# A decode-attention kernel on one core: shorter ScalarE and VectorE programs, the last V load in two pieces, 64-column pick matmuls, and the output weights in pieces of 16/8/5/2/1 and groups of eight

## The chip, the cores and the metric

The kernel runs on one core of a Trainium2 chip. The metric is device time in microseconds (us). Times are medians of several executions. All runs told here were classed as fast, so no slow-state run is compared with a fast one. The profiled execution is one of the timed ones, and its "span", the time from its first to its last instruction, is 1.4 to 2.0 us shorter than its device time. Times inside a profile count from the start of the span. A load "lands" when the profile shows its completion. The clock records here know two states of TensorE: full clock (1.00) and half clock (0.50).

## The reference, cut to what matters

```python
x: (1, 1, 512)   k_cache, v_cache: (1, 32, 16384, 128)   wq: (512, 4096)   wo: (4096, 512)   # all bf16
g = sigmoid((x * gate_w).sum(-1))
q = (x @ wq) in 32 heads of 128
a = (softmax(q k^T * 128**-0.5) v) in one row of 4096, @ wo        # per head, 16384 keys
b = gMLP(x) with w_in (512, 1792), w_out (896, 512)                # small
return g * a + (1 - g) * b                                         # one row of 512
```

One query row reads the whole of K and V: 268 MB of the 279.6 MB that the kernel moves. There is little arithmetic for each byte.

## The kernel before

K and V are loaded in sixteen pairs of heads, 8.4 MB for a K or a V load, into three big buffers of 64 KB per partition. For a pair, VectorE multiplies K by q in place in four chunks, TensorE adds up over d with an identity matrix, VectorE reduces to scores, ScalarE takes the exponentials, and TensorE multiplies with V. A load that reuses a buffer is issued only when that buffer's last user has finished.

The sizes of the pieces at the end of the stream:

```python
WG = 4                                   # rows of wo in one group of the "wide" part
TG = 8                                   # V matmuls in one group; NT = 8 groups for a pair
V_CUTS = (0, 160, 224, 256)              # last V load: pieces of 160, 64 and 32 keys per partition
WO_CUTS = (0, 16, 24, 28, 31, 32)        # wo: 16, 8, 4, 3, 1 rows per partition
WIDE = 16
```

Which buffer a load waits for (`n` counts loads; K of pair 0, K of pair 1, V of pair 0, K of pair 2, V of pair 1, ...):

```python
    for n, kind, i in loads:
        wait = [user[n - 3]] if n >= 3 else [w_free] if buf[n % 3] is setup else []
        ...
        if i == NP - 1:
            cuts, sems = (K_CUTS, ld_kh) if kind == "k" else (V_CUTS, ld_vp)
        for a, b, done in zip(cuts[:-1], cuts[1:], sems):
            sp.op(lambda e, ...: e.dma_start(...), wait=wait if a == 0 else (), inc=(done, 16))
```

V on TensorE, then the "pick" matmuls, which gather eight partial rows into two columns of the output:

```python
    def values(e, p, pa, va):
        ...
        with e.Fori(0, NT) as t:
            ...                                  # TG matmuls of 512 columns, after v_s
            fill(e, 8)
        o2 = o_ps[:, bass.ds(value(e, p, NP - 1) * 2, 2)]
        fill(e, 8, 2)
        take(e, drn_s)                           # ScalarE has drained d_ps to d_sb
        for r in range(4):
            ins = e.matmul(o2, lhsT=d_sb[:, r * Dh:(r + 1) * Dh], rhs=pick[:, r * 2:(r + 1) * 2], ...)
```

The exponentials, the drain, and the pair loop on ScalarE:

```python
    def exps(e, i):
        take(e, red_s)
        ...                                      # two Exp activations of 64x256, with sums into L_sb
    def act_pairs(e):
        e.wait_ge(*p_zero)
        exps(e, 0)
        exps(e, 1)
        with e.Fori(2, NP) as i:
            renew(e)                             # drain d_ps to d_sb, zero d_ps
            exps(e, i)
        renew(e)
        ...
```

The tail: normalise, transpose and reorder the output (VectorE and TensorE in turns), then 16 rows of wo as "wide" matmuls in a loop of WIDE / WG groups, then the other 16 rows one by one as their pieces land. (`fill` adds matmuls whose results nobody uses, to keep TensorE busy.) A piece of wo is waited for only ahead of its own rows:

```python
        with e.Fori(0, WIDE // WG) as t:
            ...                                  # WG matmuls 1x512, after wo_s
            fill(e, 1)
    for j, (a, b) in enumerate(zip(WO_CUTS[:-1], WO_CUTS[1:])):
        for k in range(max(a, WIDE), b):
            y_ok = add(o2[:, k:k + 1], wo[:, k * D:(k + 1) * D], [(ld_o[j], 16)] if k == a else (), ...)
        if b == 24:
            add(ones_f[:, 0:1], d_sb[:, :], [w_ok])     # the wide part's sum
```

The softmax here doesn't subtract the row's maximum and nothing guards it: scores larger than these inputs give would overflow.

Of the kernel before, what the change touches and what calls it, by code (L numbers as in the profile page):

```python
# [5 lines left out]
ACT = mybir.ActivationFunctionType  # L6
ALU = mybir.AluOpType
AX = mybir.AxisListType

FP32 = mybir.dt.float32  # L10
BF16 = mybir.dt.bfloat16

P = 128
Dh = 128
H = 32
NP = H // 2
# [15 lines left out]
NS = Dh // W  # L32
NG = KP // 4
TG = 8
WG = 4
NT = NG // TG
ZB = F // 4
K_CUTS = (0, 128, 256)
V_CUTS = (0, 160, 224, 256)
WO_CUTS = (0, 16, 24, 28, 31, 32)  # L40
WIDE = 16
inv_sqrt_dh = float(Dh) ** -0.5


# [132 lines left out]
def gated_mix_kernel(nc, A_x, A_k_cache, A_v_cache, A_wq, A_wo, B_x, B_w_in, B_w_sp, B_b_sp,  # L177
                     B_w_out, gate_w, out):
    def sb(name, shape, dt):
        return nc.alloc_sbuf_tensor(name, shape, dt)  # L180
# [4 lines left out]
    p_t = sb("p_t", [P, 2 * NG * 8], BF16)  # L185
    s_sb = sb("s_sb", [P, KP], FP32)
    d_sb = sb("d_sb", [P, 512], FP32)
    zero = sb("zero", [P, 512], BF16)
# [6 lines left out]
    ident = sb("ident", [P, P], BF16)  # L195
    eps_t = sb("eps_t", [P, 1], FP32)
    sel = sb("sel", [H, 4 * (P + 1)], BF16)
    pick = sb("pick", [P, 4 * 2], FP32)
    wbf = sb("wbf", [P, 2], FP32)
    g_sb = sb("g_sb", [P, 1], FP32)  # L200
    gm_sb = sb("gm_sb", [P, 1], FP32)
# [6 lines left out]
    var = sb("var", [P, 1], FP32)  # L208
    rstd = sb("rstd", [P, 1], FP32)
    u = sb("u", [P, FhC], BF16)  # L210
    L_sb = sb("L_sb", [P, H], FP32)
    rl = sb("rl", [P, H], FP32)
    o_sb = sb("o_sb", [P, H], BF16)
    oT = sb("oT", [H, P], BF16)
    o2 = sb("o2", [P, H], BF16)
# [6 lines left out]
    g_ps, t_ps = l_ps[:, 0:3], s_ps[0][:, 0:2]  # L222
# [19 lines left out]
    ld_x, ld_g, ld_q, ld_w, ld_u, st_out = (  # L242
        sem(n) for n in ("ld_x", "ld_g", "ld_q", "ld_w", "ld_u", "st_out"))
# [12 lines left out]
    pool, sp, pe, dve, act = (Queue(nc, e, n) for e, n in (  # L256
        (nc.gpsimd, "pool"), (nc.sync, "sp"), (nc.tensor, "pe"), (nc.vector, "dve"),
        (nc.scalar, "act")))


    def counter(e, name, value):
        reg = e.alloc_register(name)
        e.reg_mov(reg, value)
        return reg

    def value(e, reg, top):
        return nc.snap(bass.RegisterHandles([reg]), min_val=0, max_val=top)
# [4 lines left out]
    ident_ok = pool.chain(lambda e: e.affine_select(  # L272
        out=ident[:, :], in_=ident[:, :], compare_op=ALU.not_equal, fill=1.0, base=0,
        pattern=[[-1, P]], channel_multiplier=1))
    for t in [L_sb, p_t, zero]:
        p_zero = pool.op(lambda e, t=t: e.memset(t[:, :], 0.0), mark=True)
    pool.raw(lambda e: e.nop().then_inc(exp_s, 1))
    const_ok = dve.op(lambda e: e.memset(sel[:, :], 0.0), mark=True)


    act.op(lambda e: e.dma_start(out=x_row[:, :], in_=A_x.rearrange("b s d -> (b s) d")),
# [14 lines left out]
    for c in range(DC):  # L296
        x_ok = pe.op(lambda e, c=c: e.matmul(
            m_ps[1][:, c * P:(c + 1) * P], lhsT=x_row[0:1, c::DC], rhs=ones_row[0:1, :],
            start=True, stop=True), wait=[(ld_x, 16)] if c == 0 else (),
            mark=(c == DC - 1))  # L300
# [4 lines left out]

    act.op(lambda e: e.copy(
        out=sel[:, :].rearrange("h (i x) -> h i x", x=P + 1)[:, :, 0:P:4],
        in_=ident[0:H, 0:H].unsqueeze(1).broadcast_to([H, 4, H])), wait=[const_ok, ident_ok],
        mark=True)
    dve.op(lambda e: e.tensor_reduce(  # L310
        out=pick[:, :].rearrange("p (r s) -> p s r", r=4),
        in_=ident[:, :].rearrange("p (g x) -> p x g", x=32)[:, 0:8, :]
        .rearrange("p (s r) g -> p s r g", r=4), axis=AX.X, op=ALU.add), wait=[ident_ok], mark=True)
    dve.op(lambda e: e.tensor_tensor(out=xg_row[:, :], in0=x_row[:, :], in1=gw_row[:, :],
                                     op=ALU.mult), wait=[(ld_x, 16), (ld_g, 48)], mark=True)
    dve.op(lambda e: e.tensor_copy(out=xgw[:, 1:3], in_=wb_row[:, :]), mark=True)
    xgw_ok = dve.chain(lambda e: e.tensor_reduce(out=xgw[:, 0:1], in_=xg_row[:, :], axis=AX.X,  # L317
                                                 op=ALU.add))
# [3 lines left out]
                                    stop=True), wait=[xgw_ok], mark=True)  # L322
    act.op(lambda e: e.activation(out=g_sb[:, :], in_=g_ps[:, 0:1], func=ACT.Sigmoid),
           wait=[g_ok], mark=True)
    gm_ok = act.op(lambda e: e.activation(out=gm_sb[:, :], in_=g_ps[:, 0:1], func=ACT.Sigmoid,
                                          scale=-1.0), mark=True)
    dve.op(lambda e: e.tensor_copy(out=wbf[:, :], in_=g_ps[:, 1:3]), wait=[gm_ok], mark=True)
    g_free = dve.chain(lambda e: e.memset(g_ps, 0.0))



# [47 lines left out]
    for h in range(2):  # L379
        zh = ps_all[:, 6 * h * 512:(6 * h + 2) * 512].rearrange("p (b x) -> p b x", b=2)[:, :, 0:ZB]  # L380
        dve.op(lambda e, h=h, zh=zh: e.tensor_tensor(  # L381
            out=zm[:, 2 * h * ZB:2 * (h + 1) * ZB].rearrange("p (b m k) -> p b m k", b=2, k=FhC),
            in0=zh.rearrange("p b (m k) -> p b m k", k=FhC),
            in1=ident[:, :].rearrange("p (b m) -> p b m", b=2).unsqueeze(3).broadcast_to(
                [P, 2, 64, FhC]), op=ALU.mult), wait=[z_ok] if h == 0 else (), mark=True)
    zm_ok = (dve.sem, dve.n)
    dve.chain(lambda e: e.tensor_reduce(
        out=z[:, :].rearrange("p (e k) -> p e k", e=2),
        in_=zm.rearrange("p (e m k) -> p e k m", e=2, k=FhC), axis=AX.X, op=ALU.add))
    dve.chain(lambda e: e.scalar_tensor_tensor(  # L390
        out=zt[:, :], in0=z[:, :], scalar=0.044715, in1=z[:, :], op0=ALU.mult, op1=ALU.mult))
    zt_ok = dve.chain(lambda e: e.scalar_tensor_tensor(
        out=zt[:, :], in0=zt[:, :], scalar=1.0, in1=z[:, :], op0=ALU.add, op1=ALU.mult))
# [3 lines left out]
                  mark=True)  # L397
    dve.op(lambda e: e.tensor_tensor(out=z[:, :], in0=z[:, :], in1=zt[:, :], op=ALU.mult),
           wait=[sg_ok], mark=True)
    dve.chain(lambda e: e.tensor_reduce(out=stats[:, 0:1], in_=z[:, FhC:FC], axis=AX.X, op=ALU.add))  # L400
    dve.op(lambda e: e.tensor_tensor(out=sq[:, :], in0=z[:, FhC:FC], in1=z[:, FhC:FC],
                                     op=ALU.mult), mark=True)
    st_ok = dve.chain(lambda e: e.tensor_reduce(out=stats[:, 1:2], in_=sq[:, :], axis=AX.X,
                                                op=ALU.add))
    tot_ok = pe.op(lambda e: e.matmul(t_ps, lhsT=ones_f[:, :], rhs=stats[:, :],
                                      start=True, stop=True), wait=[st_ok], mark=True)
    dve.op(lambda e: e.tensor_scalar(out=mv[:, :], in0=t_ps, scalar1=1.0 / Fh,
                                     scalar2=0.0, op0=ALU.mult, op1=ALU.add), wait=[tot_ok],
           mark=True)
    var_ok = dve.chain(lambda e: e.scalar_tensor_tensor(  # L410
        out=var[:, :], in0=mv[:, 0:1], scalar=mv[:, 0:1], in1=mv[:, 1:2], op0=ALU.mult,
        op1=ALU.subtract))
# [6 lines left out]
                                        scalar2=wbf[:, 1:2], op0=ALU.mult, op1=ALU.add))  # L419
# [88 lines left out]
    def values(e, p, pa, va):  # L508
        v_buffer(e, va, p)
        e.reg_alu(va, va, 2 * ROW, ALU.mult)  # L510
        e.reg_alu(pa, p, 2, ALU.python_mod)
        e.reg_alu(pa, pa, 2 * NG * 8, ALU.mult)
        with e.Fori(0, NT) as t:
            p8 = p_t[:, bass.ds(t * (TG * 8), TG * 8)]
            v8 = bufs[:, bass.ds(t * (TG * 512), TG * 512)]
            n = len(nc.cur_bb.bb.instructions)
            for j in range(TG):
                ins = matmul_on(nc, e, lambda: matmul_at(
                    nc, e, d_ps, 32 * (j % 4), (8, 512), p8[:, 8 * j:8 * j + 8],
                    v8[:, j * 512:(j + 1) * 512], (p_t[:, 0:8], bufs[:, 0:512])),  # L520
                    [(va, 1024 * j), (pa, 16 * j)])
            registers_first(nc, n, lambda: take(e, v_s))
            ins.then_inc(pv_s, 1)
            fill(e, 8)
            e.reg_alu(va, va, 2 * TG * 512, ALU.add)
            e.reg_alu(pa, pa, 2 * TG * 8, ALU.add)
        o2 = o_ps[:, bass.ds(value(e, p, NP - 1) * 2, 2)]
        fill(e, 8, 2)
        take(e, drn_s)
        for r in range(4):  # L530
            ins = e.matmul(o2, lhsT=d_sb[:, r * Dh:(r + 1) * Dh],  # L531
                           rhs=pick[:, r * 2:(r + 1) * 2], start=False, stop=False,
                           skip_group_check=True)
        ins.then_inc(pe.sem, 1)

# [51 lines left out]
    def exps(e, i):  # L587
        take(e, red_s)
        at = i % 2 * (NG * 8) if isinstance(i, int) else e.snap((i & 1) * (NG * 8))
        for s in range(2):  # L590
            rows = slice(64 * s, 64 * s + 64)
            e.activation(  # L592
                out=p_t[rows, bass.ds(at, NG * 8)].rearrange("p (t c) -> p t c",
                                                             c=8)[:, :, 4 * s:4 * s + 4],
                in_=s_sb[rows, :].rearrange("p (t c) -> p t c", c=4), func=ACT.Exp,
                scale=inv_sqrt_dh, accum_out=L_sb[rows, bass.ds(i * 2 + s, 1)]).then_inc(
                    exp_s if s else act.sem, 1)
# [8 lines left out]
        e.copy(out=d_ps, in_=zero[:, :]).then_inc(drn_s, 1)  # L606

    def act_pairs(e):
        e.wait_ge(*p_zero)
        exps(e, 0)  # L610
        exps(e, 1)
        with e.Fori(2, NP) as i:  # L612
            renew(e)
            exps(e, i)
        renew(e)
        drain(e).then_inc(drn_s, 2)
        take(e, drn_s)
        e.copy(out=d_ps, in_=zero[:, :]).then_inc(act.sem, 1)
# [31 lines left out]
    def pool_pairs(e):  # L650
# [9 lines left out]
        for j, (a, b) in enumerate(zip(V_CUTS[:-1], V_CUTS[1:])):  # L660
# [3 lines left out]


    dve.op(lambda e: e.reciprocal(out=rl[:, :], in_=l_ps[:, 0:H]), wait=[(sl_s, 1)], mark=True)  # L666
    dve.chain(lambda e: e.tensor_scalar(out=rl[:, :], in0=rl[:, :], scalar1=g_sb[:, 0:1],
                                        scalar2=0.0, op0=ALU.mult, op1=ALU.add))
    o_ok = dve.chain(lambda e: e.tensor_tensor(out=o_sb[:, :], in0=o_ps[:, 0:H], in1=rl[:, :],  # L669
                                               op=ALU.mult), wait=[used_v[-1]])  # L670
    oT_ps = m_ps[1][0:H, 0:P // 2].bitcast(BF16)
    pe.raw(lambda e: warm(e, 2))
    t_ok = pe.op(lambda e: e.transpose(oT_ps, o_sb[:, :], ident[:, :]), wait=[o_ok], mark=True)
# [110 lines left out]
```

## Time and profile before

| before | |
|---|---|
| device time, median of 3 runs | 652.02 us (651.7 to 652.5) |
| span of the profiled execution | 650.2 us |
| busy: TensorE, VectorE, ScalarE | 65%, 52%, 7% |
| DMA queue of SP | 279.58 MB, 99.6% of sixteen engines' span |
| last landing of wo; end of the last matmul | 648.19; 648.54 |

These are lines of the page of the kernel before. The first two are rows of forty slices of the span: the granted TensorE clock in tenths, and the busy share of the DMA engines in tenths. The third gives packets, MB and share of sixteen engines for the queue that SP issues to. The fourth belongs to the chain of work that ended last. The fifth and sixth are groups: busy us, mean ns of one, idle time before. The last is a DMA issue: count, then the median us from issue to landing.

```profile
...
PEclk9959798958889796888969679796977969698979
DMA  9999999999999999999999999999999999999998
...
q1 hardware_dynamic: 6194, 279.58, 99.6%
...
DMA bufs<-in_A_wo_dram 4%; SPq L643 0%; PE ps_all L716 0%; DVE res L731 0%; ACT p_t L592 0%; ACTq L592 0%; ACTq L612 0%
...
L531 PE MATMUL ps_all<-pick,d_sb 128*128 128x2 f32 x128 | 17.0, 255 | 16.5 <-PEq L86 16.5
L531 PEld LDWEIGHTS ps_all<-pick,d_sb 128*128 128x128 f32 x128 | 15.7, 193 | 34.7 <-issue 34.7
...
bufs<-in_A_v_cache_dram SPq DMA_DIRECT2D x15, 31.1
```

By this page the DMA engines are busy throughout. The chain holds one large piece, a transfer of wo. The compute engines have idle time. A V load is issued 31.1 us (median) before it lands. In the trace, consecutive 8.4 MB landings lie 19.35 us apart. So the median V load has about 12 us of other transfers queued ahead of it (31.1 less its own 19.35); this is its lead.

The tail of the kernel before, from the timeline of the kernel before (start us, duration us, engine, line, what, count, idle before it and what ended it):

```profile
...
640.08 1.05 PE L531 MATMUL ps_all<-pick,d_sb 128*128 128x2 f32 x8 [0.36 <-PEq L86]
...
643.34 0.39 PE L106 MATMUL ps_all<-bufs,o 128*1 x4 [0.28 <-PEq L86]
...
645.65 0.39 PE L106 MATMUL ps_all<-bufs,o 128*1 x4 [0.19 <-PEq L86]
...
647.23 1.31 PE L716 MATMUL ps_all<-bufs,o 128*1 128x256 bf16 x16
647.94 0.38 PEld L716 LDWEIGHTS ps_all<-bufs,o 128*1 128x1 bf16 x8 [0.40 <-DMA bufs<-in_A_wo_dram]
648.61 0.36 ACT L731 CAST res<-ps_all 1x256 bf16<-1x256 f32 x1 [1.93 <-PE ps_all L716]
...
```

The wide part (L106) runs from 643.34 to 646.04 in four groups. The weight loads of the last rows wait 0.40 us for a DMA landing. TensorE is ahead of the data here, by little.

### The profile page before, as it was taken

What the parts mean: (1) busy time and instruction counts of PE and PEld (TensorE: products, weight loads), DVE (VectorE), ACT (ScalarE), POOL (GpSimd) and SP (SyncE); (2) the same over time, 40 slices, a digit from 0 to 9 for tenths busy, and PEclk for the clock granted to TensorE, in tenths of its full rate; (3) what the DMA queues carried; (4) which work ended last, traced back from release to release, by engine and by line L of the source; (5) the groups of instructions that cost most, each with busy time, mean ns of one, the idle gap of its engine ahead of it and who ended that gap; (6) DMA issues with size and microseconds to landing.
All of it is one profiled execution on the core that took longest, in us unless ns stands there. A gap on an engine that the chain in (4) does not pass through costs nothing. (4 is left out here: it accounts for less than half of the span.)

```text
span 650.2 us, 7753 instructions
## 1 busy us (share of the span) xinstructions
PE 424.3 (65%) x2474; PEld 47.0 (7%) x1312; DVE 335.8 (52%) x159; ACT 45.8 (7%) x112; POOL 2.2 (0%) x10
## 2 busy tenths in 40 slices
PE   0646687847477574857757486584748857478678
PEld 0000000000101000010000101000010100001022
DVE  3457839256380835628165370835628174465600
ACT  2210000100001000010100001000000100001011
POOL 1000000000000000000000000000000000000000
PEclk9959798958889796888969679796977969698979
DMA  9999999999999999999999999999999999999998
GB/s 384 463 419 452 452 395 443 452 443 395 452 452 395 443 452 448 391 452 452 403 435 452 448 391 452 452 431 407 452 452 395 443 452 439 399 435 468 392 428 342
DMA packets 6203, 279.60 MB, mean 430 GB/s; under 512 B 695, under 2 KB 826, under 8 KB 1210
## 3 DMA queue, kind: packets, MB, share of 16 engines
q1 hardware_dynamic: 6194, 279.58, 99.6%
q8 instruction: 1, 0.02, 0.0%
q10 hardware_dynamic: 8, 0.00, 0.0%
HBM read 279.58 MB, written 0.00 MB: 430 GB/s over the span
## 5 line engine op out<-in xcount | busy, mean ns | idle before, releaser
L579 DVE TENSOR_TENSOR bufs<-bufs,qb x64 | 281.4, 4418 | 170.8 <-DVEq L86 170.8
L91 PE MATMUL ps_all<-bufs,ident 128*128 x960 | 258.8, 423 | 0.0
L496 PE MATMUL ps_all<-bufs,ident 128*128 x64 | 28.6, 446 | 154.2 <-PEq L86 153.9
L106 PE MATMUL ps_all<-bufs,p_t 128*8 x1024 | 82.5, 396 | 30.1 <-PEq L86 20.1
L564 DVE TENSOR_REDUCE s_sb<-ps_all 128x64 f32<-128x512 f32 x64 | 44.0, 687 | 93.1 <-DVEq L86 93.1
L91 PE MATMUL ps_all<-zero,ident 128*8 128x512 bf16 (+2 forms) x167 | 59.5, 388 | 0.0
L592 ACT ACTIVATE p_t<-s_sb 64x256 f32 (+1 forms) x32 | 13.3, 415 | 433.1 <-ACTq L86 432.7
L496 PEld LDWEIGHTS ps_all<-bufs,ident 128*128 128x128 bf16 x64 | 6.3, 99 | 365.6 <-issue 365.6
L106 PEld LDWEIGHTS ps_all<-bufs,p_t 128*8 x1024 | 19.4, 83 | 163.1 <-issue 161.6
L531 PE MATMUL ps_all<-pick,d_sb 128*128 128x2 f32 x128 | 17.0, 255 | 16.5 <-PEq L86 16.5
L531 PEld LDWEIGHTS ps_all<-pick,d_sb 128*128 128x128 f32 x128 | 15.7, 193 | 34.7 <-issue 34.7
L601 ACT COPY d_sb<-ps_all 128x512 f32<-128x512 f32 x16 | 9.4, 586 | 105.4 <-ACTq L86 105.4
L606 ACT CAST ps_all<-zero 128x512 f32<-128x512 bf16 x15 | 8.8, 589 | 1.7
L666 DVE RECIPROCAL rl<-ps_all 128x32 f32<-128x32 f32 x1 | 0.4, 357 | 12.2 <-PE ps_all L552 12.2
L381 DVE TENSOR_TENSOR bufs<-ps_all,ident 128x896 f32<-128x896 f32 x2 | 2.1, 1086 | 8.6 <-PE ps_all L91 8.6
L669 DVE TENSOR_TENSOR o_sb<-ps_all,rl 128x32 bf16<-128x32 f32 x1 | 0.2, 191 | 11.5 <-PE ps_all L531 11.5
L592 ACT ACTIVATION_READ_ACCUMULATOR p_t<-s_sb (+1 forms) x32 | 5.9, 185 | 0.0
L321 PE MATMUL ps_all<-xgw,const-float32-1.0 1*128 1x3 f32 x2 | 0.6, 360 | 8.0 <-DVE xgw L317 8.0
L91 PE MATMUL ps_all<-bufs,xb 128*128 x12 | 5.0, 552 | 0.0
L106 PE MATMUL ps_all<-bufs,u 128*1 x14 | 2.6, 372 | 3.1 <-ACT ps_all L427 2.4
L345 PE MATMUL ps_all<-bufs,xb 128*128 x4 | 2.3, 574 | 3.3 <-DMA bufs<-in_B_w_in_dram 3.3
L106 PE MATMUL ps_all<-bufs,xb 128*64 x32 | 3.6, 380 | 0.0
(76 smaller groups left out, 40.2 us busy)
## 6 DMA issues: line engine op xcount, KB each, us to landing
bufs<-in_A_k_cache_dram SPq DMA_DIRECT2D x2, 4096.0 KB, 36.2
bufs<-in_A_v_cache_dram SPq DMA_DIRECT2D x1, 5120.0 KB, 34.5
bufs<-in_A_wq_dram SPq DMA_DIRECT2D x1, 4096.0 KB, 12.3
bufs<-in_A_v_cache_dram SPq DMA_DIRECT2D x1, 2048.0 KB, 39.0
bufs<-in_A_wo_dram SPq DMA_DIRECT2D x1, 2048.0 KB, 25.4
bufs<-in_B_w_in_dram SPq DMA_DIRECT2D x1, 1792.0 KB, 15.5
bufs<-in_A_v_cache_dram SPq DMA_DIRECT2D x1, 1024.0 KB, 41.0
bufs<-in_A_wo_dram SPq DMA_DIRECT2D x1, 1024.0 KB, 27.6
```

Source lines behind the costliest of these rows:

```text
L91: ins = eng.matmul(out, lhsT=lhsT, rhs=rhs, **flags).ins
L106: ins = eng.matmul(bank[0:m, 0:n], lhsT=lhsT, rhs=rhs, **flags).ins
L321: g_ok = pe.op(lambda e: e.matmul(g_ps, lhsT=ones_f[0:1, :], rhs=xgw[:, :], start=True, stop=True), wait=[xgw_ok], mark=True)
L345: if n else matmul_on(nc, e, lambda: e.matmul(args[0], lhsT=args[1], rhs=args[2], **flags), [at, (xa, 0)]))
L381: dve.op(lambda e, h=h, zh=zh: e.tensor_tensor(out=zm[:, 2 * h * ZB:2 * (h + 1) * ZB].rearrange("p (b m k) -> p b m k", b=2, k=FhC), in0=z ...
L496: matmul_on(nc, e, lambda: e.matmul(s3, lhsT=ident[:, :], rhs=k3[:, :, 0:W], start=True, **flags), [(kw, 0)])
L531: ins = e.matmul(o2, lhsT=d_sb[:, r * Dh:(r + 1) * Dh], rhs=pick[:, r * 2:(r + 1) * 2], start=False, stop=False, skip_group_check=True)
L564: return e.tensor_reduce(out=s_sb[:, c * QK:(c + 1) * QK], in_=s_ps[c % 2].rearrange("p (j w) -> p j w", w=W), axis=AX.X, op=ALU.add)
L579: e.tensor_tensor(out=k3, in0=k3, in1=qi, op=ALU.mult).then_inc(mul_s, 1)
L592: e.activation(out=p_t[rows, bass.ds(at, NG * 8)].rearrange("p (t c) -> p t c", c=8)[:, :, 4 * s:4 * s + 4], in_=s_sb[rows, :].rearrange(" ...
L601: return e.copy(out=d_sb[:, :], in_=d_ps)
L606: e.copy(out=d_ps, in_=zero[:, :]).then_inc(drn_s, 1)
```

## The change

The author wants fewer instructions on ScalarE and VectorE, fewer pieces at the end, and less loop overhead in the wide part. Cut to its core:

```diff
-WG = 4
+WG = 8
-V_CUTS = (0, 160, 224, 256)
-WO_CUTS = (0, 16, 24, 28, 31, 32)
+V_CUTS = (0, 192, 256)
+WO_CUTS = (0, 16, 24, 29, 31, 32)
+PW = 64
-    pick = sb("pick", [P, 4 * 2], FP32)
+    pick = sb("pick", [P, 4 * PW], FP32)          # columns 2 to 63 are zero
-    const_ok = dve.op(lambda e: e.memset(sel[:, :], 0.0), mark=True)
+    dve.op(lambda e: e.memset(pick[:, :], 0.0), mark=True)      # sel: now a POOL memset
-    dve.op(lambda e: e.tensor_copy(out=wbf[:, :], in_=g_ps[:, 1:3]), wait=[gm_ok], mark=True)
+    wbf_ok = act.op(lambda e: e.copy(out=wbf[:, :], in_=g_ps[:, 1:3]), mark=True)
-        o2 = o_ps[:, bass.ds(value(e, p, NP - 1) * 2, 2)]
+        o2 = o_ps[:, bass.ds(value(e, p, NP - 1) * 2, PW)]
     def act_pairs(e):
-        exps(e, 0)
-        exps(e, 1)
-        with e.Fori(2, NP) as i:
-            renew(e)
-            exps(e, i)
+        e.activation(out=var[:, :], in_=eps_t[:, :], func=ACT.Exp)   # loads the Exp table early
+        ...                                  # one copy of renew and exps, entered by branches
-    dve.chain(lambda e: e.tensor_scalar(out=rl[:, :], in0=rl[:, :], scalar1=g_sb[:, 0:1], ...))
-    o_ok = dve.chain(lambda e: e.tensor_tensor(out=o_sb[:, :], in0=o_ps[:, 0:H], in1=rl[:, :], ...))
+    o_ok = dve.chain(lambda e: e.scalar_tensor_tensor(
+        out=o_sb[:, :], in0=o_ps[:, 0:H], scalar=g_sb[:, 0:1], in1=rl[:, :], op0=ALU.mult, ...))
```

## The prediction

> **What bounds it now.** DMA, nearly throughout. The page's forty slices show DMA at 9 all along; the SP queue's 279.6 MB fill 99.6% of sixteen engines' span. Read packet by packet, each engine runs without a gap until 647.1 to 647.7 us (64 KB take 2.42 us, 8 KB 0.313, 1 KB 0.046). The chain of waits has one large piece, a 28.9 us transfer of wo. TensorE (65%), VectorE (52%) and ScalarE (7%) have room. The table of DMA issues shows 31 to 41 us from issue to landing of K and V loads, which themselves need about 19, so buffers come free in time. Only bytes, packets and what follows the last landing count: last wo row 648.19, TensorE ends 648.54, copies 649.02, span 650.2.
>
> **What the change does.**
> 1. Head (memsets moved, wbf copy on ScalarE, Exp table loaded early): engines have gaps of 5 us there, and the first V load, issued at 36.2 us, has about 17 us of transfers queued before it. Worth 0.
> 2. ScalarE loop rewritten, two VectorE operations fused (0.24 us saved, in a 12 us wait). Worth 0.
> 3. Last V in two pieces: eight packets fewer per DMA engine, about 7 ns each from the packet times: -0.07 us, on the critical path. But the second piece leaves two groups of eight matmuls after it, and the first lands later, estimated at 633.3 from landings at 630.9 and 635.7. TensorE issues a group per 0.9 us, so the last starts at about 639.7 instead of 638.3: o2 comes 1.4 us later, 2 at half clock. [...] (stretches are multiples of 3.41 us; 630.1 to 637.0 was at half clock). [...]
> 4. pick with 64 columns: its passes are paced by weight loads (0.97 us of 1.05); an fp32 pass of 256 columns costs 0.107 us here, so 64 about 0.03, hidden. Worth 0.
> 5. Wide wo part in 2 groups of 8: before, four groups took 0.77 us each (643.2 to 646.0); a group of eight takes about 0.9, so 1.2 us is won, most of what step 3 loses.
> 6. wo tail 5/2/1 for 4/3/1: less work between the last two landings, but the one-row landing already decided (TensorE waited for it). 0 to -0.05.
>
> **Sum.** -0.07 us of DMA; 0 to +0.6 if TensorE's backlog from step 3 outlasts the last landing. One 16 KB instruction fetch, at 647.3 on a DMA engine that had just finished, may move onto a busy one: up to +0.6. In all -0.3 to +0.7, against a spread of 0.8 us over the three runs.
>
> Predicted: **652.0 us**, 651.2 to 653.0. Faster by over 2%: 0.5%; within 2%: 99%; slower: 0.5%.
>
> **What would show it.** The DMA row stays 9, 279.6 MB, and the chain of waits is still one wo transfer of about 29 us. pick matmuls of the last pair start 1 to 2 us later than 640.08; the wide part starts near 644 and ends near 646; the last matmuls follow the last landing by under 0.4 us. If TensorE is busy without a pause through its last 2 us, step 3 cost time. A mean of pick matmuls well over 0.3 us refutes step 4.
>
> **What would make it wrong.** [...] more skew between the sixteen engines; a stall at the start that shifts the first transfers; a half-clock tail.

The sum came to -0.3 to +0.7 us on the 652.02 us read for the kernel before. Its terms are estimates. For the "up to +0.6" of the instruction fetch the trace of the kernel before has these figures: a 16 KB data packet takes 0.615 us, the 16 KB fetch took 1.10 us.

## The result, and the profile after

The kernel after takes 651.75 us (median of 6 runs, 651.61 to 652.1), the kernel before 651.68 us (6 runs, 651.54 to 652.5). The ratio is 1.0, with a 95% interval of 0.9987 to 1.0012. Ratios and intervals here are from means of fast runs, so not quite the ratio of the medians quoted.

The page of the kernel after, the same lines:

```profile
...
PEclk9959788968879697897969879796987968699978
DMA  9999999999999999999999999999999999999998
...
q1 hardware_dynamic: 6050, 279.58, 99.5%
...
DMA bufs<-in_A_wo_dram 5%; SPq L654 0%; DVE res L741 0%; PE ps_all L726 0%; ACT p_t L594 0%; ACTq L594 0%; ACTq L622 0%; ACTq L621 0%
...
L533 PE MATMUL ps_all<-pick,d_sb 128*128 128x64 f32 x128 | 17.6, 280 | 16.5 <-PEq L87 16.5
L533 PEld LDWEIGHTS ps_all<-pick,d_sb 128*128 128x128 f32 x128 | 15.5, 191 | 34.8 <-issue 34.8
...
```

There are 144 packets fewer (128 of data, 16 completion writes), the bytes are the same, and the DMA row is the same. The pick passes grew by 25 ns each, while their weight loads, which pace them (0.97 us of the last eight's 1.05 before and 1.10 after), did not (193 ns, then 191).

The timeline of the kernel after, its tail:

```profile
...
641.69 1.10 PE L533 MATMUL ps_all<-pick,d_sb 128*128 128x64 f32 x8 [0.36 <-PEq L87]
...
644.63 0.60 PE L107 MATMUL ps_all<-bufs,o 128*1 x8
...
645.42 0.60 PE L107 MATMUL ps_all<-bufs,o 128*1 x8
...
647.29 1.41 PE L726 MATMUL ps_all<-bufs,o 128*1 128x256 bf16 x16
647.97 0.09 PEld L726 LDWEIGHTS ps_all<-bufs,o 128*1 128x1 bf16 x4 [0.26 <-DMA bufs<-in_A_wo_dram]
648.42 0.08 PEld L726 LDWEIGHTS ps_all<-bufs,o 128*1 128x1 bf16 x2 [0.37 <-DMA bufs<-in_A_wo_dram]
648.77 0.36 ACT L741 CAST res<-ps_all 1x256 bf16<-1x256 f32 x1 [2.10 <-PE ps_all L726]
...
```

The pick matmuls came 1.61 us later than before (641.69 against 640.08). The wide part started 1.29 us later and ended at 646.03, where it had ended before (646.04): two groups took 1.40 us where four took 2.70. From then on the two tails are alike. TensorE waits for the last landings of wo, and the last matmul ends 0.35 us (before) and 0.32 us (after) behind the last landing, at 648.19 and 648.38.

This leaves two questions. Did the parts cancel, or was there slack everywhere (time in which TensorE would have waited for data anyway)? And where do the runs of one kernel that are up to a microsecond slower come from?

### The profile page after: what moved, and what is told of

The parts are those of the page before. It is cut to its first block, busy times and chain, and to the rows that moved or that the text cites. A ratio compares the mean times of both kernels' runs of the same rounds, so it can differ in the third digit from the quotient of the medians.

```text
span 650.4 us, 7767 instructions
## 1 busy us (share of the span) xinstructions
PE 430.8 (66%) x2472; PEld 46.2 (7%) x1312; DVE 335.8 (52%) x157; ACT 46.0 (7%) x114; POOL 2.6 (0%) x11
## 5 line engine op out<-in xcount | busy, mean ns | idle before, releaser
L92 PE MATMUL ps_all<-bufs,ident 128*128 x960 | 266.4, 434 | 0.0
L498 PE MATMUL ps_all<-bufs,ident 128*128 x64 | 28.8, 449 | 145.2 <-PEq L87 144.9
L92 PE MATMUL ps_all<-zero,ident 128*8 128x512 bf16 (+1 forms) x165 | 58.5, 387 | 0.0
L594 ACT ACTIVATE p_t<-s_sb 64x256 f32 x32 | 13.3, 415 | 461.4 <-ACTq L87 461.0
L533 PE MATMUL ps_all<-pick,d_sb 128*128 128x64 f32 x128 | 17.6, 280 | 16.5 <-PEq L87 16.5
L594 ACT ACTIVATION_READ_ACCUMULATOR p_t<-s_sb x32 | 5.9, 184 | 0.0
```

The lines of the kernel that those rows point to most:

```text
L92: ins = eng.matmul(out, lhsT=lhsT, rhs=rhs, **flags).ins
L498: matmul_on(nc, e, lambda: e.matmul(s3, lhsT=ident[:, :], rhs=k3[:, :, 0:W], start=True, **flags), [(kw, 0)])
L594: e.activation(out=p_t[rows, bass.ds(at, NG * 8)].rearrange("p (t c) -> p t c", c=8)[:, :, 4 * s:4 * s + 4], in_=s_sb[rows, :].rearrange(" ...
```

## The experiments

Twelve kernels ran in three groups, each group beside the kernel before on the same chip. All passed the comparison with the reference, even the one that is wrong on purpose in two of 32 heads.

### The two-piece V alone, and the wider groups alone

```diff
-V_CUTS = (0, 160, 224, 256)
+V_CUTS = (0, 192, 256)
```

> The kernel before with the last V in two pieces, nothing else changed. Theory (the DMA stream sets the time; the two pieces push TensorE's last chain back by about 1.6 us and the wider wo groups absorb it): last pick matmuls at about 641.7 us, wide wo part from 644.6 in four groups of 0.77 us, so TensorE has 16+4+8+6+2 matmuls of backlog when the last wo row lands at 648.2, ends at about 650.1 instead of 648.54 and never waits for the last two landings. Time 1.0 to 1.6 us above before (ratio about 1.002). Rival (the tail has slack enough by itself, the wider groups do nothing): last matmuls still within 0.4 us of the last landing, time within 0.3 us of before.

```diff
-WG = 4
+WG = 8
```

> The kernel before with the wide wo part in two groups of eight, nothing else changed. Theory: TensorE is through with the wide part 1.0 to 1.2 us earlier and waits longer for wo landings; the last matmuls follow the last landing by 0.35 us as before; time within 0.3 us of before. Rival (the wide part is on the critical path in before and the change gains there what the V pieces lose): 0.5 to 1.2 us faster than before.

```diff
-V_CUTS = (0, 192, 256)          # in the kernel after
+V_CUTS = (0, 160, 224, 256)
```

> The changed kernel with the last V in three pieces again. Theory: pick matmuls of the last pair at about 640.1 us (1.6 earlier than in the changed kernel), more waiting for wo landings, same end: time within 0.3 us of before and of the changed kernel, last matmuls within 0.4 us of the last landing. Rival (the two pieces cost the changed kernel time that other parts win back): 0.5 to 1.5 us faster than the changed kernel.

```diff
-WG = 8                          # in the kernel after
+WG = 4
```

> The changed kernel with the wide wo part in four groups of four again. Theory: the TensorE backlog of the two-piece V is no longer absorbed: wide part from about 644.6 to 647.7 us, TensorE ends about 1.3 to 1.6 us after where the last landing would let it, time 1.0 to 1.6 us above before. Rival (tail has slack without the wider groups): within 0.3 us of before.

| kernel (5 runs each; before: 652.04, 9 runs, 651.58 to 652.27) | median | all runs | ratio |
|---|---|---|---|
| before, V in two pieces | 652.76 | 652.35 to 653.62 | 1.0013 (1.0 to 1.0027) |
| before, wo groups of eight | 651.67 | 651.45 to 652.18 | 0.9994 (0.9981 to 1.0008) |
| after, V in three pieces | 651.91 | 651.71 to 652.73 | 1.0002 (0.9988 to 1.0015) |
| after, wo groups of four | 652.66 | 652.35 to 653.6 | 1.0011 (0.9998 to 1.0025) |

The two kernels that join two V pieces with groups of four are the slow ones, by 0.6 to 0.7 us of the medians. The intervals touch 1.0 or hold it, so these ratios alone would not prove it. The tail does. This is the timeline of the kernel before with V in two pieces:

```profile
...
642.64 1.05 PE L531 MATMUL ps_all<-pick,d_sb 128*128 128x2 f32 x8 [0.36 <-PEq L86]
...
647.69 0.39 PE L106 MATMUL ps_all<-bufs,o 128*1 x4 [0.19 <-PEq L86]
...
649.05 0.96 PEld L716 LDWEIGHTS ps_all<-bufs,o 128*1 128x1 bf16 x16
649.27 1.04 PE L716 MATMUL ps_all<-bufs,o 128*1 128x256 bf16 x16
650.37 0.36 ACT L731 CAST res<-ps_all 1x256 bf16<-1x256 f32 x1 [1.66 <-PE ps_all L716]
...
```

All sixteen weight loads of the last rows stand in one block with no wait for DMA. The last wo row landed at 648.82 and the last matmul ended at 650.31, which is 1.49 us behind it instead of 0.35. The kernel after with groups of four shows the same: 648.77 and 650.34. With V in three pieces and groups of eight, TensorE has slack and gains nothing: the last matmul ends 0.32 us behind the landing, and the time stays. (The two-piece kernel and the kernel after with groups of four had been expected to lose 1.0 to 1.6 us; the medians lost less.)

So the groups of eight win back what the two V pieces cost, 0.6 to 0.7 us of the medians, and win nothing where the V pieces are three. The change took slack away in one place and gave it back in another.

One thing did not fit. In the profile of the two-piece kernel the last landing itself is 0.6 us later than in the kernel before, and the same holds for the groups of eight alone (648.77), which have no reason for it.

### The tail parts without the shorter programs, and narrow pick

The first kernel is the kernel before with the four tail parts only (V, WG, WO_CUTS, pick):

> The kernel before with only the tail parts of the change (V in two pieces, wo groups of eight, wo 5/2/1, 64-column pick): the ScalarE loop, the Exp table, the moved memsets, the wbf copy and the fused VectorE operation stay as before. Theory (shorter programs are off the critical path): same time as the changed kernel and as before within 0.3 us, one 16 KB instruction fetch as in both. Rival (the shorter programs win what the two V pieces cost): 0.5 us or more slower than before, or more instruction fetches than one.

```diff
-PW = 64                         # in the kernel after
+PW = 2
```

> The changed kernel with pick matmuls of 2 columns again. Theory (weight loads pace them): the eight passes of the last pair take 1.05 instead of 1.10 us, mean about 255 ns instead of 280, time the same within 0.3 us. Rival (64 columns keep TensorE at full clock and so help the tail): a lower granted clock around the pick matmuls and a later end of the wide wo part by 0.5 us or more.

Measured beside a before of 651.74 us (9 runs, 651.57 to 652.96): tail parts only 652.74 us (651.78 to 652.87, ratio 1.0006, 0.9992 to 1.002); narrow pick 651.85 us (651.7 to 653.12, ratio 1.0003, 0.999 to 1.0017).

The narrow pick decides its question. The tile's own view, in the kernel after and then with two columns (duration min/median/max in ns):

```profile
...
L533 PE MATMUL ps_all<-pick,d_sb x128: 275/275/318, 99.8 to 642.5; 128*128 128x64 f32 x128
...
```

```profile
...
L533 PE MATMUL ps_all<-pick,d_sb x128: 251/251/344, 99.3 to 642.3; 128*128 128x2 f32 x128
...
```

64 columns cost 24 ns a pass at the median, 0.05 us for the last eight together (their passes overlap: eight of 275 ns in 1.10 us), and the clock around them is no better for it: the full clock comes at 636.96 with two columns and at 637.60 with 64.

The tail parts alone did not decide: the median is 1.0 us slower than before, the interval holds 1.0, and one run of five (651.78) is as fast as any. Its profile shows a last landing at 648.64 and a TensorE backlog of 0.68 us behind it. There was one 16 KB instruction fetch, as in all profiles. This had to wait for the last group.

### Delaying ScalarE, and taking bytes away

```diff
     def exps(e, i):
         take(e, red_s)
+        for _ in range(10):
+            e.copy(out=idle[:, :], in_=zero[:, :]).then_inc(idle_s, 1)
+            take(e, idle_s)
```

> The changed kernel with ten extra ScalarE copies (0.59 us each, near 7 us with their semaphores) ahead of every pair's exponentials. Theory (DMA-bound; V loads are queued 12 us before the queue would run dry): issue to landing of V loads shrinks from about 31 to about 24 us, the DMA row stays at 9, time within 0.5 us of before. Rival (ScalarE's length matters through buffers that come free late): 16 pairs make it several us to 100 us slower.

```diff
+        if i == NP // 2 and kind == "v":
+            cuts = (0, KP // 2)           # half of one V load; wrong result on purpose
```

> Wrong result on purpose: the changed kernel loads only the first half of one middle V buffer (4.19 MB less); all compute is kept. Theory (DMA sets the time): 4.19 MB at the measured 430 GB/s is 9.75 us, so about 642.0 us, a ratio of 0.985. Rival (compute or the buffers' turnover has an equal share of the bound): well under half of that.

The half load: 643.89 us (643.71 to 644.7), ratio 0.9875 (0.986 to 0.989). That is 7.9 us saved of the 9.75 expected, so DMA sets the time, but not with the whole of the bytes. The landings tell where most of the rest went. The half load landed 9.71 us after its forerunner instead of 19.35, and the second load after it came 1.54 us late. It had been issued at 393.71 us, only 2.6 us before the load ahead of it landed. The shorter load had eaten the lead that later loads live on.

The delay of ScalarE was the miss: 662.66 us (662.1 to 663.43), ratio 1.0168 (1.0152 to 1.0183), where at most 0.5 us had been expected. The steady state behaved nearly as expected: the median V load still landed 23.9 us after its issue. These are windows of the DMA in the delayed kernel and in the kernel after (us, busy time and count of PE, PEld, DVE, ACT and POOL, clock, DMA share, GB/s):

```profile
...
90.00:100.00 10.00, 7.99 (x65) 0.84 (x49) 4.88 (x3) 4.11 (x7) 0.00 (x0) 1.00 0.49 210
...
```

```profile
...
90.00:100.00 10.00, 7.23 (x76) 1.31 (x67) 4.05 (x2) 2.19 (x6) 0.00 (x0) 1.00 0.99 426
...
```

The queue ran dry for long only once, between 90 and 110 us. The second V load (pair 1) landed 29.05 us after the load ahead of it instead of 19.35. This one gap of 9.7 us is nearly all of the 10.1 us that the span grew. Later loads lost 0.3 us at most each. So one load had little lead, and no median shows it.

### The second V load

All profiles so far can be asked when that load was issued, and how long after its forerunner it landed. The lines are from the timeline of SP in the kernel before, in the kernel after, and in the kernel before with V in two pieces:

```profile
...
90.87 0.33 SPq L638 DMA_DIRECT2D bufs<-in_A_v_cache_dram  x1
...
```

```profile
...
91.56 0.33 SPq L649 DMA_DIRECT2D bufs<-in_A_v_cache_dram  x1
...
```

```profile
...
92.31 0.33 SPq L638 DMA_DIRECT2D bufs<-in_A_v_cache_dram  x1
...
```

| profiled execution of | second V issued, us | its landing after the one ahead, us |
|---|---|---|
| before | 90.87 | 19.35 |
| after, pick of 2 columns | 91.06 | 19.35 |
| after, V in three pieces | 91.37 | 19.35 |
| after | 91.56 | 19.35 |
| after, half a V load | 92.09 | 19.54 |
| before, V in two pieces | 92.31 | 20.21 |
| before, wo groups of eight | 92.34 | 20.05 |
| after, wo groups of four | 92.50 | 20.17 |
| before, tail parts only | 92.76 | 19.82 |
| after, ScalarE delayed | 103.23 | 29.05 |

Up to 91.56 us nothing is lost. From 92.09 to 92.76 there is a loss of 0.2 to 0.9 us, not strictly in order, although such an issue stands about 3 us before the transfers ahead of it end (95.2 to 95.6 us in the two-piece kernel). With nothing queued, at the start of the kernel before, the first packet starts 1.01 us after its issue begins and 0.63 us after it ends. The loss happens in the first packets of that load: in the two-piece kernel they start on time, at 95.2 to 95.6 us, but nine of the sixteen take 2.44 to 3.48 us where a 64 KB packet takes 2.42 (median of the kernel before). All later landings, the last wo row too, are late by most of that. It explains the late last landing of the groups of eight alone, and why that profiled execution, at 652.18 us, was the slowest of its five.

The load waits for the exponentials of the second K pair. These wait for score sums on TensorE, which run at half or full clock: in the kernel after, fifteen sums from 69.73 us, most of them at half clock, took 5.72 us where fifteen at full clock took 3.40. In the clock records of the kernels before and after every whole stretch at one clock is a multiple of 3.41 us (3.41, 6.83, 17.07 and others). Where these steps fall, their phase, differs between executions: full clock for the tail starts at 636.95 us in the kernel before and at 637.60 in the kernel after. Three of the profiles happen to have the same phase by the author's reading, and they issued this load at 92.31, 92.34 and 92.50; the timelines of the first two agree (eleven sums from 83.65 and 83.69 us took 3.69 and 3.67 us). Two share another phase (full clock for the tail from 636.95 and 636.96 us) and issued it at 90.87 and 91.06. This is a correlation. No run set the phase.

So the last group gave the load a lead. The first K load was split in halves, so that VectorE can begin about 5 us earlier:

```diff
-        if i == NP - 1:
+        if i == NP - 1 or (i == 0 and kind == "k"):
             cuts, sems = (K_CUTS, ld_kh) if kind == "k" else (V_CUTS, ld_vp)
...
-        hand(e, ld_k[0], k_s, 2)
+        for j in range(len(ld_kh)):
+            hand(e, ld_kh[j], k_s, 1)
```

> The changed kernel with the first K load split in halves, each with its own completion, so that VectorE starts about 5 us earlier. Theory (the slow runs of every version come from the second V load: it is issued when the second K buffer has been used, between 90.9 and 92.8 us as TensorE's clock phase has it, and past about 92 us the sixteen queues run dry, by up to 0.9 us, once): the second V load is issued at about 86 us, every load lands 19.35 us after the one before, and all five times lie between 651.4 and 652.1. Rival (the slow runs have another cause): spread of a microsecond or more as in the runs so far.

> The kernel before with the same split of the first K load. Theory: as for the changed kernel with it, the time within 0.2 us of that one's, no run over 652.2.

> The kernel before with the last V in two pieces and the first K load split. Theory: without the stall at the second V load, what is left is TensorE's backlog in the tail alone, 1.0 to 1.6 us over the kernel before with the split; the last matmuls end 1.2 us or more after the last landing. Rival (the 0.7 us that this kernel lost without the split was the stall): within 0.3 us of the kernel before with the split.

> The kernel before with all the tail parts of the change and the first K load split. Theory (the shorter programs win nothing, and the 652.7 of the tail parts alone was the stall plus a late full clock): within 0.3 us of the changed kernel with the split. Rival (the shorter programs win 0.5 us or more): slower than the changed kernel with the split by that much.

The same line in the timeline of SP, kernel after with the split:

```profile
...
86.66 0.33 SPq L649 DMA_DIRECT2D bufs<-in_A_v_cache_dram  x1
```

The tails of the two slower ones with the split, first the kernel before with V in two pieces (groups of four), then the tail parts alone (groups of eight):

```profile
...
641.85 1.05 PE L531 MATMUL ps_all<-pick,d_sb 128*128 128x2 f32 x8 [0.36 <-PEq L86]
...
648.26 0.96 PEld L717 LDWEIGHTS ps_all<-bufs,o 128*1 128x1 bf16 x16
...
649.59 0.36 ACT L732 CAST res<-ps_all 1x256 bf16<-1x256 f32 x1 [1.67 <-PE ps_all L717]
...
```

```profile
...
642.20 1.10 PE L533 MATMUL ps_all<-pick,d_sb 128*128 128x64 f32 x8 [0.36 <-PEq L87]
...
647.45 1.01 PEld L719 LDWEIGHTS ps_all<-bufs,o 128*1 128x1 bf16 x16
...
648.77 0.36 ACT L734 CAST res<-ps_all 1x256 bf16<-1x256 f32 x1 [1.60 <-PE ps_all L719]
...
```

| first K load split in (5 runs each; before without it: 652.15, 9 runs, 651.64 to 652.52) | median | all runs | ratio to before | last landing, last matmul's end |
|---|---|---|---|---|
| after | 651.89 | 651.74 to 652.24 | 0.9999 (0.9985 to 1.0012) | 648.33, 648.64 |
| before | 651.74 | 651.61 to 651.88 | 0.9996 (0.9982 to 1.001) | 648.23, 648.58 |
| before, V in two pieces | 652.36 | 652.31 to 652.61 | 1.0005 (0.9992 to 1.0019) | 648.19, 649.52 |
| before, tail parts only | 652.29 | 651.72 to 652.37 | 1.0001 (0.9988 to 1.0015) | 648.34, 648.71 |

In all four the load was issued at 84.9 to 86.7 us, and the steps around it were 19.34 to 19.36 us. In none of these profiles was there a stall, that is, a gap before the second V load's landing. The spread of the two-piece kernel fell from 1.27 to 0.30 us, that of the kernel before to 0.27 us beside 0.88 without the split on the same chip. For the kernel after the expectation was missed: one run took 652.24 us where at most 652.1 had been expected, and its spread of 0.50 us is what it was without the split (0.49).

So the second V load isn't the whole answer. With the split the spans of one kernel differ by 0.2 to 0.4 us; without it those of the two-piece kernel differed by 1.3, of the tail parts alone by 0.8, of the kernel before by 0.5 to 0.9, of the kernel after by 0.5. Another part of the spread lies outside the span. In kernels with the old ScalarE and VectorE programs the device time is 1.4 to 1.5 us over the span in 35 of 57 runs and 1.7 to 2.0 us in 22; in kernels with the shorter ones it is 1.5 to 1.7 us in all 34. The cause of that stays open.

With the stall gone, the two-piece V with groups of four costs 0.62 us of the medians, and none of its times (from 652.31) reaches those of the kernel before with the split (up to 651.88). In the profiled execution the last matmul ends 1.33 us behind the landing. The expected cost of 1.0 to 1.6 us was too high for the median. The mechanism stands, the size was smaller.

A rival for this backlog is the clock, whose full state comes at different moments in different executions. The lines above and the clock records speak against it: in these two profiles the tail parts alone reached full clock later (638.56 us against 637.97) and their pick matmuls came later (642.20 against 641.85), but with groups of eight the last matmul ends only 0.37 us behind the landing. (The two also differ in pick and in the last wo pieces; the kernels above that change the groups alone agree.) The clock is not without weight, though. Here the last weight loads no longer wait for DMA, so the slack is used up, and in the profile without the split, at full clock from 639.46 us, the backlog was 0.68 us.

The tail parts alone, with the split, are 0.40 us slower than the whole change with it. That lies between what the two theories expected (up to 0.3, from 0.5), and one run of the five (651.72) is as fast as the fastest of the whole change (651.74). The medians of the spans are 650.4 and 650.3 us, so most of the 0.40 us lies outside the span, where four of the five runs of the tail parts spend 1.8 to 2.0 us. Inside the span no worth of the shorter programs is seen beyond that 0.1 us, which the runs' own 0.4 us covers; whether they are worth a few tenths outside it is left open.

## Why the prediction was right or wrong

The time was right: 652.0 us predicted, 651.75 measured, in the range. The kernel before had been read as 652.02 us then and measured 651.68 beside the change, so how close the two numbers are is in part luck. That no difference would show was argued from DMA, and that held. Point by point:

- **DMA bounds it.** Right. The DMA row, bytes and chain were as said, and 4.19 MB less made the kernel 7.9 us faster.
- **Step 1, "Worth 0", and "buffers come free in time".** The net of the head was indeed not seen in the result, but the reason was wrong. The first V load has the lead that the prediction read (17 us) and more: the load ahead of it landed 21 us after its issue. The second was issued only 5 us before the load ahead of it landed, and the prediction judged it by the median of fifteen loads. The runs show instead that an issue at 92.1 to 92.8 us cost 0.2 to 0.9 us, and one at 103.23 us, with ScalarE delayed by 7.5 us a pair, 9.7 us. So a change of the head that moves this issue can cost or win there.
- **Step 2, the ScalarE loop and the fused operation.** No worth is shown. The fused VectorE operation takes 0.25 us on the tail's chain where the plain product took 0.19; the saved one lay in a wait. Inside the span 0.1 us, less than the spread, as said above; outside it open to a few tenths.
- **Step 3.** Right. The pick matmuls came 1.61 us later (predicted 1.4 to 2). The -0.07 us of DMA cannot be told from the spread: the mean end of the data on the sixteen DMA engines, pieced together from the packets, stayed near 647.4 us and came about 0.03 us earlier. The half-clock range is real too: the full clock came 4.0 us after the first group of the last V in the kernel after, 5.9 us in the kernel before, with TensorE busy throughout both stretches (4.02 and 5.91 us).
- **Step 4.** Right: 280 ns instead of 255 on average, the weight loads unchanged at 0.97 us for the last eight, no time gained or lost by itself.
- **Step 5.** Right, and a little better than said: 1.30 us won. The two V pieces need it, as the kernels with groups of four show; by how much may depend on the clock (a backlog of 0.37 us with full clock from 638.56 us, 0.68 with full clock from 639.46).
- **Step 6.** Right in the kernel after, where the weight loads wait 0.37 us for the one-row landing. In the kernel before it was a tie: they waited 0.10 us, and the last row's matmuls started 0.11 us after those ahead of them, like the row before. No run changed this alone.
- **"May move onto a busy one".** The 16 KB instruction fetch moved from 647.32 to 647.79 us, right behind the last completion write of all; in both kernels it started within 6 ns of the end of a completion write. It took 1.10 us before and 1.07 us after, 0.93 to 1.44 us over all profiles. The last landing was seen 0.59 us after the end of that write. In the other thirteen profiles, where the fetch came elsewhere or later, this took 0.42 to 0.46 us. So it probably cost 0.15 us in this execution. No run set it on purpose.

No version here beats both kernels. The kernel before with the first K load split has the steadiest times (651.61 to 651.88, five runs), but its interval against the kernel before holds 1.0.

## What to carry to other kernels

Where DMA is saturated (99.6% of sixteen engines' span here), ask of each change only two things: does it alter what the queues carry, and does compute still finish before the last landing. A part that takes slack and a part that gives it back belong together, and only undoing them one at a time shows it. Judge the lead of loads by the worst one, not by the median. Here it was among the first: one load in over thirty explained up to 0.9 us of the slow profiled executions, which looked like noise. Compare spans as well as times before giving the whole of a spread to one cause: about half a microsecond lay outside the span here.
